# Loading an expert's input weights as bf16 from GpSimd's queue, and holding two loads of x until the band sums are taken

## The chip, the cores and the metric

The kernel runs on one core of one Trainium2 chip. A core has TensorE (matrix products into PSUM), VectorE, ScalarE and GpSimd (elementwise work), SyncE (which here issues transfers), and 16 DMA engines that all queues share. The metric is the time of one execution on the device, in microseconds: the median over three runs of the kernel before is 724.11 (723.76 to 725.01). The profiled execution spans 721.8 us.

## The reference

The input x is 8 x 4096 x 192 in fp32, the convolution's weights are 8 x 7, w_in is 192 x 2048 and w_out 2048 x 192. What is computed:

```
w    = softmax(weight, axis=-1)                  # 8 heads x 7 taps
y[s] = sum over k of w[head, k] * x[s + k - 6]   # causal, per head of 24 columns, zeros before each sequence
h    = y @ w_in                                  # 32768 x 2048
g    = h * cos(h)
out  = g @ w_out                                 # 32768 x 192, fp32
```

## The kernel before

Tokens are handled in units of 1024 (`U`), read in blocks of 128, and in tiles of 512 (`T`), two tiles to a unit. For a unit the steps are: load x as fp32 (`load_unit`, L72, with `load_edges`, L68, for the rows that reach back into earlier blocks); cast it to bf16 on GpSimd (`cast_unit`, L179); convolve it on TensorE by a product with a banded matrix `band` (L194; L292 for the first half of unit 0); copy the result out of PSUM as `ct`, doubled along its columns (L209, L251, or at once in L298); and turn it so that the 192 columns of the model lie on partitions (`cT`), by a transposing transfer on SyncE (L257), or for the first half of unit 0 by TensorE against an identity (L314, L317).

For a tile, eight steps j of matmul 1 (`mm1`, L350) multiply cT by a pair of blocks of 128 columns of w_in (`w`, bf16), ScalarE takes the cosine (L357), VectorE multiplies (L361), and matmul 2 (L380) works with w_out (`wo`, bf16) and `g`. The two halves of w_in's columns lie on partitions 0 to 63 and 64 to 127, and the two matmuls of a step use one half of TensorE's rows each. Outputs are copied by ScalarE (L392) and stored by SyncE.

The order of the work on each engine is written out by hand: `manual_schedule()` keeps the order of the program, and the strings `PE_FIRST`, `PE_ORDER`, `ACT_FIRST` and `ACT_ORDER` (L403 to L408) set how steps of matmul 1 (`h0` to `h7`), pieces of convolution (`c`, `d`, and `r` for `conv_rest`) and steps of matmul 2 (`m`) follow one another in a tile. Each engine[...] works strictly in the order of issue. A `nop` on SyncE with a dependence (L302) makes the transfers behind it wait for the named instruction.

The opening, which the change touches, goes like this before it:

- SyncE issues the first half of unit 0's x, then the first half of w_in in fp32 (`load_w(0)`, L84), then the second half of unit 0. ScalarE issues the second half of w_in (L118) and later unit 1 with its edges (L150, L151).
- TensorE runs products with zeros (`keep_warm`, L106) and spreads the convolution's weights to all partitions (L122). VectorE and ScalarE take the softmax of them (L145 to L156).
- GpSimd makes a mask of 32 partitions by two instructions (L130, L131) and copies it three times to the other partitions (L134). It then clears a block of `xb0`, and makes the identity (L137 to L140).
- VectorE multiplies mask and weights (`prod`, L270) and sums over the taps (`diag`, L273): these are the band sums. Sixteen small copies on three engines (L278) put them into `band`.
- ScalarE casts the first half of unit 0. TensorE convolves it (`conv_first`), and it is turned (`turn_first`). When its last copy is done, SyncE issues w_out in four transfers (L94).
- GpSimd casts the first quarter of w_in to bf16 (L280) as soon as it has landed, casts the second half of unit 0 (L281), casts the other three quarters of w_in (L334), and casts unit 1 (L335).
- The loop over tiles follows. In tile 0, `conv_rest` convolves the second half of unit 0; `double_unit` and `turn_unit` finish it, and then SyncE issues the load of unit 2 (L445) and GpSimd casts w_out in two pieces (L448).

Of the kernel before, what the change touches and what calls it, by code (L numbers as in the profile page):

```python
# [8 lines left out]
FP32 = mybir.dt.float32  # L9
BF16 = mybir.dt.bfloat16  # L10
AF = mybir.ActivationFunctionType
ALU = mybir.AluOpType
# [4 lines left out]
def kernel(  # L17
# [8 lines left out]
    nc = tc.nc  # L26
# [7 lines left out]
    NB = T // 128  # L34
    U = 1024
    NU = NTOK // U
    UB = U // 128
# [3 lines left out]
    NP = NF // 2  # L41
    NC = D // 64
# [4 lines left out]
    consts = ctx.enter_context(tc.tile_pool(name="consts", bufs=1))  # L47
# [20 lines left out]
    def load_edges(u, queue=nc.sync):  # L68
        queue.dma_start(out=x_tiles[u][:, UB, :],
                          in_=xf[u * U - 8 : u * U - 8 + U, :].rearrange("(n t) d -> n t d", t=128)[:, 0:16, :])  # L70

    def load_unit(u, n0=0, n1=UB, queue=nc.sync):  # L72
        if n0 == 0:
            x_tiles[u] = xin.tile([128, UB + 1, D], FP32, name="x_f")
        queue.dma_start(out=x_tiles[u][:, n0:n1, :],  # L75
                          in_=xf[u * U + n0 * 128 : u * U + n1 * 128, :].rearrange("(n p) d -> p n d", p=128))


    w_f = consts.tile([128, NC, NP, 128], FP32)
    w_src = moe_w_in.rearrange("(m k) (t f) -> t m k f", k=NC, t=2)  # L80
    HP = NP // 2

    def load_w(t, queue):
        queue.dma_start(out=w_f[64 * t : 64 * t + 64].rearrange("p k j f -> p k (j f)"), in_=w_src[t])  # L84

    load_unit(0, 0, NB)
    load_w(0, nc.sync)
    load_unit(0, NB, UB)
    wo_f = consts.tile([128, NP, 2, D], FP32)
    wo_src = moe_w_out.rearrange("(i j p) d -> p j i d", i=2, p=128)  # L90

    def load_wo(q):
        for i in range(2):
            nc.sync.dma_start(out=wo_f[:, q * HP : (q + 1) * HP, i], in_=wo_src[:, q * HP : (q + 1) * HP, i])  # L94
# [9 lines left out]
    def keep_warm(n, bank=idle):  # L104
        for _ in range(n):
            nc.tensor.matmul(out=bank, lhsT=zero[:, 0:128], rhs=zero, start=True, stop=True)  # L106
# [7 lines left out]
                            channel_multiplier=32)  # L114
    scrap = consts.tile([128, 1], FP32)
    nc.scalar.activation(out=scrap, in_=one, func=AF.Exp)  # L116

    load_w(1, nc.scalar)  # L118
    keep_warm(3)
    w_all = o_pools[1].tile([128, T], FP32, name="o_ps1")  # L120
    w_bc = w_all[:, 0 : HQ * K].rearrange("p (h k) -> p h k", k=K)
# [7 lines left out]
    mask = consts.tile([128, E, K], BF16)  # L129
    nc.gpsimd.memset(mask[0:32], 0.0)  # L130
    nc.gpsimd.affine_select(out=mask[0:32], in_=mask[0:32], compare_op=ALU.not_equal, fill=1.0, base=1 - K,  # L131
                            pattern=[[1, E], [1, K]], channel_multiplier=-1)
    for q in range(1, 4):
        nc.gpsimd.tensor_copy(out=mask[32 * q : 32 * q + 32], in_=mask[0:32])  # L134
    band = consts.tile([128, H, 256], BF16)
    nc.vector.memset(band, 0.0)
    nc.gpsimd.memset(xb0[:, 0, :], 0.0)  # L137
    ident = consts.tile([128, 128], BF16)
    nc.gpsimd.memset(ident, 0.0)
# [7 lines left out]
    nc.vector.tensor_tensor(out=wexp, in0=w_bc, in1=wmax.to_broadcast([128, HQ, K]), op=ALU.subtract)  # L147
    nc.scalar.activation(out=wexp, in_=wexp, func=AF.Exp)
    nc.scalar.activation(out=scrap, in_=one, func=AF.Sin)
    load_unit(1, queue=nc.scalar)  # L150
    load_edges(1, queue=nc.scalar)  # L151
    wsum = consts.tile([128, HQ, 1], FP32)
    nc.vector.tensor_reduce(out=wsum[:, :, 0], in_=wexp, axis=mybir.AxisListType.X, op=ALU.add)
    winv = consts.tile([128, HQ, 1], FP32)
    nc.vector.reciprocal(winv, wsum)
    nc.vector.tensor_tensor(out=wn, in0=wexp, in1=winv.to_broadcast([128, HQ, K]), op=ALU.mult)  # L156
    w = consts.tile([128, NC, NP, 128], BF16)
    wo = consts.tile([128, NP, 2, D], BF16)


    sync_dep = mybir.DependencyInfo(mybir.DependencyClass.Sync, mybir.DependencyReason.DATA)
# [17 lines left out]
    def cast_unit(u, n0=0, n1=UB + 1, copy=nc.gpsimd.tensor_copy):  # L179
        bf[u] = xb0 if u == 0 else xbf_pool.tile([128, UB + 1, D], BF16, name="x_bf")  # L180

        o = 1 if u == 0 else 0
        copy(out=bf[u][:, n0 + o : n1 + o, :].rearrange("p n (h k r) -> p (n h) k r", k=NC, r=R),  # L183
             in_=x_tiles[u][:, n0:n1, :].rearrange("p n (h r k) -> p (n h) k r", k=NC, r=R))
        if u and u % UPS == 0:
            nc.gpsimd.memset(bf[u][0:8, UB, :], 0.0)
        bf.pop(u - 2, None)
# [27 lines left out]
    def o_banks():  # L215
        return [o_pools[b].tile([128, T], FP32, name="o_ps%d" % b) for b in range(2)]
# [52 lines left out]
    prod = consts.tile([128, HQ, E, K], BF16)  # L269
    nc.vector.tensor_tensor(out=prod, in0=mask.rearrange("p (o e) k -> p o e k", o=1).to_broadcast([128, HQ, E, K]),  # L270
                            in1=wn.rearrange("p h (o k) -> p h o k", o=1).to_broadcast([128, HQ, E, K]), op=ALU.mult)
    diag = consts.tile([128, HQ, E], FP32)
    nc.vector.tensor_reduce(out=diag, in_=prod, axis=mybir.AxisListType.X, op=ALU.add)  # L273

    three = {"D": nc.vector.tensor_copy, "A": nc.scalar.copy, "P": nc.gpsimd.tensor_copy}
    for i, k in enumerate("DPDPDPADPDPADPAD"):
        q, rows = divmod(i, 4)
        three[k](out=band[32 * rows : 32 * rows + 32, HQ * q : HQ * (q + 1), 32 * rows : 32 * rows + E],  # L278
                     in_=diag[32 * q : 32 * q + 32])
    nc.gpsimd.tensor_copy(out=w[:, :, 0:2], in_=w_f[:, :, 0:2])  # L280
    cast_unit(0, NB, UB)  # L281
    ct_tiles[0] = ct_pool.tile([128, UB + 1, NC, 2, 64], BF16, name="ct")
    cT[0] = cT_pool.tile([128, UB + 1, NC, 128], BF16, name="cT")
# [2 lines left out]
    def conv_first():  # L286

        banks = o_banks()
        for half in range(2):
            for h in range(H):  # L290
                for prev in range(2):
                    nc.tensor.matmul(  # L292
                        out=banks[half][:, 0 : 2 * D].rearrange("p (n k h r) -> p h n k r", n=2, k=NC, h=H)[:, h],
                        lhsT=band[:, h, 128 * prev : 128 * prev + 128],
                        rhs=bf[0][:, 2 * half + 1 - prev : 2 * half + 3 - prev, h * G : (h + 1) * G].rearrange(
                            "p n (k r) -> p n k r", k=NC),
                        start=(h == 0 and prev == 0), stop=(h == H - 1 and prev == 1), skip_group_check=True)
            m = copies[half](out=ct_tiles[0][:, 2 * half : 2 * half + 2].rearrange("p n k t w -> p (n k) t w"),  # L298
                             in_=banks[half][:, 0 : 2 * D].rearrange("p (m t w) -> p m t w", t=1, w=64).to_broadcast(
                                 [128, 2 * NC, 2, 64]))  # L300

        tc.add_manual_dep(nc.sync.nop().ins, m.ins.name, sync_dep, reason="order of the transfers")  # L302
        load_wo(0)
        load_wo(1)

    def turn_first(half):
        for n in range(2):
            last = half and n
            ps = [o_pools[0].tile([128, T], FP32, name="o_ps0")] if last else ring_banks()
            if n == 0:  # L310
                keep_warm(2 - half, ps[1])
            ps = ps[0]
            for k in range(NC):
                nc.tensor.matmul(out=ps[:, k * 128 : (k + 1) * 128],  # L314
                                 lhsT=ct_tiles[0][:, 2 * half + n, k, :, :].rearrange("p t w -> p (t w)"), rhs=ident,
                                 start=True, stop=True, skip_group_check=True)
            copies[n](out=cT[0][:, 2 * half + n].rearrange("p c k -> p (c k)"), in_=ps[:, 0 : NC * 128])  # L317

    def conv_rest():
# [6 lines left out]
        for b in range(2):  # L326
            for c in range(2):
                conv_out(0, c, [x[:, 4 * G * 2 * c :] for x in banks], NB, NB, UB, copies[1 - b], banks=(b,))

    conv_first()  # L330
    turn_first(0)
    turn_first(1)
    for j in (2, 4, 6):
        nc.gpsimd.tensor_copy(out=w[:, :, j : j + 2], in_=w_f[:, :, j : j + 2])  # L334
    cast_unit(1)  # L335


# [181 lines left out]
```

## Time and profile before

| What | Value |
|---|---|
| Median of three runs | 724.11 us |
| Span of the profiled execution | 721.8 us |
| TensorE busy | 709.3 us, 98% |
| VectorE busy | 611.2 us, 85% |
| ScalarE busy | 617.0 us, 85% |
| GpSimd busy | 152.6 us, 21% |
| Moved by transfers | 86.03 MB, mean 119 GB/s |
| Cast of w_in's first quarter (L280), starts at | 12.58 us |
| First product of matmul 1 (L350), starts at | 13.46 us |
| Cast of unit 1 (L183), starts at | 18.09 us |
| Load of unit 2 issued (L75), at | 23.04 us |

All times within a profile count from the start of its span. A line of the timeline gives start, length, engine, source line, operation, what it writes and reads with shapes, how many instructions are merged in it, and in brackets how long the engine had been idle before and what released it. A line of the chain gives start, length and the piece of work: the chain is followed back from the last instruction, at each step to what released it. A line of the stretches gives a window, then for each engine its busy time with the number of instructions, then the clock that TensorE was granted (1.00 is full), the share of the 16 DMA engines that was busy, and the GB/s that they moved. PE is TensorE, PEld its weight loads, DVE VectorE, ACT ScalarE, POOL GpSimd, SPq the queue of SyncE.

### The profile page before, as it was taken

The page shows a single profiled execution, that of the slowest core. Times are in us where ns is not written, and L with a number is a line of the kernel's source. Part 1 is how long each engine was busy: PE and PEld are TensorE (multiplying, and loading weights), DVE is VectorE, ACT ScalarE, POOL GpSimd, SP SyncE. Part 2 cuts the span into 40 slices and gives each one's busy share as a digit, 9 for nine tenths or more (in the row PEclk, how much of TensorE's full clock was granted, in tenths as well). Part 3 has the DMA queues.
Part 4 walks back from the last instruction along what each step waited for, and adds up shares of the span by engine and source line. Part 5 has one row for each costly group of instructions (what it writes and reads, how often), then busy time and mean ns, then how long its engine had stood idle before and what let it go on. Part 6 is the DMA issues. An engine that isn't in the chain of part 4 may idle for free.

```text
span 721.8 us, 26319 instructions
## 1 busy us (share of the span) xinstructions
PE 709.3 (98%) x11826; PEld 530.9 (74%) x11827; DVE 611.2 (85%) x535; ACT 617.0 (85%) x779; POOL 152.6 (21%) x129
## 2 busy tenths in 40 slices
PE   7899999999999999999999999999999999999997
PEld 3577777777777777777777777777777777777776
DVE  5878888888888888888888888888888888888884
ACT  5888888888888888888888888888888888888884
POOL 5731122210222210222210222210222211221000
PEclk9999999999999999999999999999999999999999
DMA  9855434555443556444555343566443555324312
GB/s 232 206 123 144 106 111 94 123 144 143 104 113 92 126 143 141 97 123 91 127 144 139 104 116 89 130 144 131 109 119 86 135 143 131 108 74 81 87 46 67
DMA packets 183665, 86.03 MB, mean 119 GB/s; under 512 B 111617, under 2 KB 183169, under 8 KB 183553
## 3 DMA queue, kind: packets, MB, share of 16 engines
q1 hardware_dynamic: 182160, 82.69, 47.1%
q10 hardware_dynamic: 1392, 1.67, 0.9%
q8 instruction: 92, 1.51, 0.9%
q14 instruction: 21, 0.16, 0.1%
HBM read 31.36 MB, written 25.17 MB: 78 GB/s over the span
## 4 chain that ended last, share of the span: by engine, by line
PE 95%; DMA 2%; POOL 1%; issue 0%; SPq 0%; ACT 0%; DVE 0%; DVEq 0%; POOLq 0%
PE o_ps L380 46%; PE h L350 45%; PE h L194 3%; DMA x_f<-in_x_dram 2%; POOL x_bf L183 1%; PE h L380 0%; POOL w L334 0%; POOL wo L448 0%; SPq L75 0%; DVE g L361 0%; DVEq L514 0%; ACT cs L357 0%; ACT o_sb L392 0%; POOL ct L251 0%; SPq L84 0%
## 5 line engine op out<-in xcount | busy, mean ns | idle before, releaser
L361 DVE TENSOR_TENSOR g<-h,cs 128x1024 bf16<-128x1024 f32 (+1 forms) x513 | 603.6, 1218 | 97.2 <-ACT cs L357 92.3
L357 ACT ACTIVATE cs<-h 128x1024 bf16<-128x1024 f32 (+1 forms) x513 | 511.6, 1026 | 63.0 <-PE h L350 55.8
L380 PE MATMUL o_ps<-wo,g 64*128 64x192 bf16 x8128 | 423.8, 243 | 1.7 <-ACT o_sb L392 0.6
L380 PEld LDWEIGHTS <-g 64*128 64x128 bf16 x8192 | 362.2, 94 | 86.0 <-SPq L168 1.2
L350 PE MATMUL h<-cT,w 64*128 64x512 bf16 (+1 forms) x3078 | 399.5, 377 | 3.4 <-POOL w L280 3.3
L350 PEld LDWEIGHTS <-w 64*128 64x128 bf16 x3078 | 155.0, 94 | 88.8 <-POOL w L280 3.5
L263 POOL COPY cT<-cT 128x144 bf16<-128x144 bf16 x31 | 9.5, 307 | 495.5 <-DMA cT<-ct 392.0
L183 POOL CAST x_bf<-x_f 128x1728 bf16<-128x1728 f32 (+1 forms) x32 | 80.6, 2518 | 4.7 <-DMA x_f<-in_x_dram 4.4
L209 ACT CAST ct<-h 128x432 bf16<-128x432 f32 x120 | 56.4, 522 | 27.8 <-PE h L194 27.2
L392 ACT COPY o_sb<-o_ps 128x384 f32<-128x384 f32 x127 | 60.2, 474 | 4.9 <-PE o_ps L380 4.9
L251 POOL COPY ct<-ct 128x1728 bf16<-128x1728 bf16 (+1 forms) x32 | 51.3, 1603 | 19.4 <-ACT ct L209 19.1
L194 PE MATMUL h<-x_bf,band 64*128 64x216 bf16 (+1 forms) x472 | 42.7, 254 | 1.0 <-POOL x_bf L183 1.0
L194 PEld LDWEIGHTS <-band 64*128 64x128 bf16 (+1 forms) x496 | 22.5, 95 | 6.4 <-issue 3.8
L106 PE MATMUL o_ps<-zero 128*128 128x512 bf16 x12 | 5.3, 610 | 1.3 <-DVE zero L101 1.3
L380 PE MATMUL h<-wo,g 64*128 64x192 bf16 x64 | 5.8, 243 | 0.0
L106 PEld LDWEIGHTS <-zero 128*128 128x128 bf16 x15 | 1.7, 127 | 3.6 <-issue 2.2
L194 PE MATMUL o_ps<-x_bf,band 128*128 128x96 bf16 (+1 forms) x24 | 2.3, 253 | 1.3 <-POOL x_bf L183 1.3
L448 POOL CAST wo<-wo_f 128x1536 bf16<-128x1536 f32 x2 | 2.9, 1476 | 0.0
L209 ACT CAST ct<-o_ps 128x432 bf16<-128x432 f32 (+1 forms) x6 | 2.4, 461 | 0.2
L116 ACT ACT_TABLE_LOAD x1 | 1.3, 1283 | 1.4 <-PEq L503 1.4
L392 ACT COPY o_sb<-h 128x384 f32<-128x384 f32 x1 | 0.5, 478 | 2.4 <-PE h L380 2.4
L334 POOL CAST w<-w_f 128x768 bf16<-128x768 f32 x3 | 2.4, 832 | 0.0
(47 smaller groups left out, 27.8 us busy)
## 6 DMA issues: line engine op xcount, KB each, us to landing
out_dram<-o_sb SPq DMA_DIRECT2D x63, 384.0 KB
x_f<-in_x_dram SPq DMA_DIRECT2D x30, 768.0 KB
x_f<-in_x_dram SPq DMA_DIRECT2D x30, 96.0 KB
wo_f<-in_moe_w_out_dram SPq DMA_DIRECT2D x4, 384.0 KB
x_f<-in_x_dram SPq DMA_DIRECT2D x2, 384.0 KB
w_f<-in_moe_w_in_dram SPq DMA_DIRECT2D x1, 768.0 KB
w_f<-in_moe_w_in_dram ACTq DMA_DIRECT2D x1, 768.0 KB
x_f<-in_x_dram ACTq DMA_DIRECT2D x1, 768.0 KB
```

The lines of the kernel that those rows point to most:

```text
L106: nc.tensor.matmul(out=bank, lhsT=zero[:, 0:128], rhs=zero, start=True, stop=True)
L183: copy(out=bf[u][:, n0 + o : n1 + o, :].rearrange("p n (h k r) -> p (n h) k r", k=NC, r=R), in_=x_tiles[u][:, n0:n1, :].rearrange("p n (h ...
L194: return nc.tensor.matmul(out=ps[i // 2][:, 0 : (n1 - n0) * 2 * G].rearrange("p (n k i r) -> p i n k r", n=n1 - n0, k=NC, i=2)[:, i % 2], ...
L209: copy(o[:, :, 0, :], i[:, :, 0, :])
L251: nc.gpsimd.tensor_copy(out=ct[:, n0:n1, :, 1, :], in_=ct[:, n0:n1, :, 0, :])
L263: nc.gpsimd.tensor_copy(out=cT[u][:, 0:UB, :, 0 : K - 1], in_=cT[u][:, UB].rearrange("p c (n t) -> p n c t", t=16)[:, :, :, 8 : 8 + K - 1])
L350: nc.tensor.matmul(out=h[:, i, n0 * 128 : n1 * 128], lhsT=w[rows, k, j, :], rhs=c[rows, m0 + n0 : m0 + n1, k, :], start=(k == 0), stop=(k ...
L357: nc.scalar.activation(out=cs[:, :, part], in_=h[:, :, part], func=AF.Sin, bias=math.pi / 2.0, scale=1.0)
L361: nc.vector.tensor_tensor(out=g_tiles[t][:, 2 * j : 2 * j + 2, part], in0=h[:, :, part], in1=cs[:, :, part], op=ALU.mult)
L380: m = nc.tensor.matmul(out=o_ps[tt, b][:, si * D : (si + 1) * D], lhsT=g_tiles[tt][rows, f, s * 128 : (s + 1) * 128], rhs=wo[rows, f // 2, ...
L392: nc.scalar.copy(o_sb[t][:, 2 * b : 2 * b + 2, :].rearrange("p s d -> p (s d)"), o_ps.pop((t, b))[:, 0 : 2 * D])
L448: nc.gpsimd.tensor_copy(out=wo[:, q * HP : (q + 1) * HP], in_=wo_f[:, q * HP : (q + 1) * HP])
```

## The change

It changes how the opening's transfers are made and ordered:

- `w` is loaded straight as bf16 by two transfers on GpSimd's queue, which read fp32 from memory and write bf16; the fp32 tile `w_f` and its four casts on GpSimd (L280, L334) go.
- The three copies of the mask go from GpSimd to VectorE (one) and ScalarE (two), so that GpSimd reaches its transfers sooner.
- The second half of unit 0, unit 1 and its edges are all issued by SyncE, and only after the band sums (a `nop` on SyncE that depends on the sum of L273), so that the bytes of w_in go ahead of them.

Line numbers in the text are those of the kernel before.

```diff
--- before.py
+++ after.py
@@ -76,16 +76,15 @@
                           in_=xf[u * U + n0 * 128 : u * U + n1 * 128, :].rearrange("(n p) d -> p n d", p=128))
 
 
-    w_f = consts.tile([128, NC, NP, 128], FP32)
+
+    w = consts.tile([128, NC, NP, 128], BF16)
     w_src = moe_w_in.rearrange("(m k) (t f) -> t m k f", k=NC, t=2)
     HP = NP // 2
 
-    def load_w(t, queue):
-        queue.dma_start(out=w_f[64 * t : 64 * t + 64].rearrange("p k j f -> p k (j f)"), in_=w_src[t])
+    def load_w(t):
+        nc.gpsimd.dma_start(out=w[64 * t : 64 * t + 64].rearrange("p k j f -> p k (j f)"), in_=w_src[t])
 
     load_unit(0, 0, NB)
-    load_w(0, nc.sync)
-    load_unit(0, NB, UB)
     wo_f = consts.tile([128, NP, 2, D], FP32)
     wo_src = moe_w_out.rearrange("(i j p) d -> p j i d", i=2, p=128)
 
@@ -114,8 +113,6 @@
                             channel_multiplier=32)
     scrap = consts.tile([128, 1], FP32)
     nc.scalar.activation(out=scrap, in_=one, func=AF.Exp)
-
-    load_w(1, nc.scalar)
     keep_warm(3)
     w_all = o_pools[1].tile([128, T], FP32, name="o_ps1")
     w_bc = w_all[:, 0 : HQ * K].rearrange("p (h k) -> p h k", k=K)
@@ -130,10 +127,12 @@
     nc.gpsimd.memset(mask[0:32], 0.0)
     nc.gpsimd.affine_select(out=mask[0:32], in_=mask[0:32], compare_op=ALU.not_equal, fill=1.0, base=1 - K,
                             pattern=[[1, E], [1, K]], channel_multiplier=-1)
-    for q in range(1, 4):
-        nc.gpsimd.tensor_copy(out=mask[32 * q : 32 * q + 32], in_=mask[0:32])
     band = consts.tile([128, H, 256], BF16)
     nc.vector.memset(band, 0.0)
+    for q, copy in enumerate((nc.vector.tensor_copy, nc.scalar.copy, nc.scalar.copy)):
+        copy(out=mask[32 * q + 32 : 32 * q + 64], in_=mask[0:32])
+    for t in range(2):
+        load_w(t)
     nc.gpsimd.memset(xb0[:, 0, :], 0.0)
     ident = consts.tile([128, 128], BF16)
     nc.gpsimd.memset(ident, 0.0)
@@ -147,14 +146,11 @@
     nc.vector.tensor_tensor(out=wexp, in0=w_bc, in1=wmax.to_broadcast([128, HQ, K]), op=ALU.subtract)
     nc.scalar.activation(out=wexp, in_=wexp, func=AF.Exp)
     nc.scalar.activation(out=scrap, in_=one, func=AF.Sin)
-    load_unit(1, queue=nc.scalar)
-    load_edges(1, queue=nc.scalar)
     wsum = consts.tile([128, HQ, 1], FP32)
     nc.vector.tensor_reduce(out=wsum[:, :, 0], in_=wexp, axis=mybir.AxisListType.X, op=ALU.add)
     winv = consts.tile([128, HQ, 1], FP32)
     nc.vector.reciprocal(winv, wsum)
     nc.vector.tensor_tensor(out=wn, in0=wexp, in1=winv.to_broadcast([128, HQ, K]), op=ALU.mult)
-    w = consts.tile([128, NC, NP, 128], BF16)
     wo = consts.tile([128, NP, 2, D], BF16)
 
 
@@ -270,14 +266,18 @@
     nc.vector.tensor_tensor(out=prod, in0=mask.rearrange("p (o e) k -> p o e k", o=1).to_broadcast([128, HQ, E, K]),
                             in1=wn.rearrange("p h (o k) -> p h o k", o=1).to_broadcast([128, HQ, E, K]), op=ALU.mult)
     diag = consts.tile([128, HQ, E], FP32)
-    nc.vector.tensor_reduce(out=diag, in_=prod, axis=mybir.AxisListType.X, op=ALU.add)
+    summed = nc.vector.tensor_reduce(out=diag, in_=prod, axis=mybir.AxisListType.X, op=ALU.add)
+
+    tc.add_manual_dep(nc.sync.nop().ins, summed.ins.name, sync_dep, reason="order of the transfers")
+    load_unit(0, NB, UB)
+    load_unit(1)
+    load_edges(1)
 
     three = {"D": nc.vector.tensor_copy, "A": nc.scalar.copy, "P": nc.gpsimd.tensor_copy}
     for i, k in enumerate("DPDPDPADPDPADPAD"):
         q, rows = divmod(i, 4)
         three[k](out=band[32 * rows : 32 * rows + 32, HQ * q : HQ * (q + 1), 32 * rows : 32 * rows + E],
                      in_=diag[32 * q : 32 * q + 32])
-    nc.gpsimd.tensor_copy(out=w[:, :, 0:2], in_=w_f[:, :, 0:2])
     cast_unit(0, NB, UB)
     ct_tiles[0] = ct_pool.tile([128, UB + 1, NC, 2, 64], BF16, name="ct")
     cT[0] = cT_pool.tile([128, UB + 1, NC, 128], BF16, name="cT")
@@ -298,7 +298,6 @@
             m = copies[half](out=ct_tiles[0][:, 2 * half : 2 * half + 2].rearrange("p n k t w -> p (n k) t w"),
                              in_=banks[half][:, 0 : 2 * D].rearrange("p (m t w) -> p m t w", t=1, w=64).to_broadcast(
                                  [128, 2 * NC, 2, 64]))
-
         tc.add_manual_dep(nc.sync.nop().ins, m.ins.name, sync_dep, reason="order of the transfers")
         load_wo(0)
         load_wo(1)
@@ -330,8 +329,6 @@
     conv_first()
     turn_first(0)
     turn_first(1)
-    for j in (2, 4, 6):
-        nc.gpsimd.tensor_copy(out=w[:, :, j : j + 2], in_=w_f[:, :, j : j + 2])
     cast_unit(1)
 
 
```

## The prediction

> **What bounds the kernel now.** I read the page's busy shares, then the chain of work that ended last, then the stretches of the first 23 us, then the order of instructions in them.
>
> ```profile
> PE 709.3 (98%) x11826; PEld 530.9 (74%) x11827; DVE 611.2 (85%) x535; ACT 617.0 (85%) x779; POOL 152.6 (21%) x129
> ...
> PE 95%; DMA 2%; POOL 1%; issue 0%; SPq 0%; ACT 0%; DVE 0%; DVEq 0%; POOLq 0%
> ```
>
> TensorE carries 95% of the chain. The change touches none of its matmuls, so it is worth what it moves the opening, where the chain is not on TensorE. In order of time that part reads (start, length, what):
>
> ```profile
> 2.06 12.51 DMA x_f<-in_x_dram
> 14.57 0.05 issue
> 14.62 1.22 POOL x_bf L183
> 15.84 1.53 POOL w L334 x2
> 17.38 0.72 issue
> 18.09 0.99 POOL x_bf L183
> ...
> 20.57 0.84 POOL ct L251
> ...
> 23.04 0.86 SPq L75
> ...
> 23.95 5.34 DMA x_f<-in_x_dram
> ...
> 29.44 2.54 POOL x_bf L183
> ...
> 32.02 0.53 PE h L194 x4
> ```
>
> Unit 0's second half lands at 14.57, GpSimd casts it, then casts three quarters of w_in (L334), then casts unit 1, doubles unit 0's ct, and only then can SyncE turn unit 0 and load unit 2 (23.04), which ends in the convolution at 32.02. From there TensorE runs nearly without a gap: whatever shifts 32.02 shifts the end. Beside it lies a second chain, which starts at w_in:
>
> ```profile
> 12.58 0.82 POOL L280 CAST w<-w_f 128x768 bf16<-128x768 f32 x1 [4.84 <-DMA w_f<-in_moe_w_in_dram]
> ...
> 13.46 2.73 PE L350 MATMUL h<-cT,w 64*128 64x256 bf16 x18 [3.29 <-POOL w L280]
> 14.30 1.24 ACT L357 ACTIVATE cs<-h 128x512 bf16<-128x512 f32 x2 [3.79 <-PE h L350]
> ```
>
> The last of w_in is in at about 12.55; with the first cast, matmul 1 starts at 13.46, though cT was ready near 10.5. Both chains wait for bytes. The stretches (engine columns, then granted clock, DMA share, GB/s) show how these flow:
>
> ```profile
> 4.00:8.00 4.00, 3.67 (x23) 1.47 (x22) 3.42 (x12) 3.33 (x6) 2.62 (x10) 1.00 1.00 210
> 8.00:12.00 4.00, 2.06 (x34) 1.27 (x35) 2.08 (x3) 1.75 (x3) 0.00 (x0) 1.00 1.03 225
> 12.00:20.00 8.00, 5.93 (x52) 3.18 (x53) 3.90 (x6) 4.63 (x8) 6.20 (x6) 0.79 1.09 312
> 20.00:23.00 3.00, 2.32 (x20) 1.09 (x19) 2.67 (x3) 2.92 (x6) 3.00 (x4) 1.00 0.15 35
> ```
>
> The DMA engines are full from 3 to 20 us. While w_in's 4 KB packets pass they move 210 to 225 GB/s; once only rows of x and w_out (768 B) are left, 312. The clock's 0.79 hides 0.50 between 14 and 16 us, after TensorE's idle 3.29.
>
> **What the skill says.** (1) "DMA: Bandwidth & Descriptors", section "SWDGE vs HWDGE vs iDMA": a cast in transit must be issued from GpSimd, whose cores write the descriptors in software. No transfer before is of that kind. (2) Same page, "Anatomy of one DMA": about 2.0 us fixed plus bytes at 436 GB/s; "Specifications" puts the first byte about 1 us after issue. (3) "SBUF — State Buffer", section "Door 1: The DMA port swizzle": a destination of 64 partitions reaches half the ports, 196 GB/s measured at 1 MiB, and two such transfers side by side gain little. The 210 of w_in's stretch agrees, so the writing side may set its pace. (4) "TensorE: Matmul & The Clock Gate", "What's actually happening": about 3.4 us of idle halves the clock. The trace agrees (3.29 idle, then 0.50).
>
> **The change, part by part.**
>
> Removed from GpSimd: four casts of w_in, 0.82 + 2.38 us (L280, L334), both on the chains above, and three mask copies (1.29 us, L134).
>
> Mask copies: one on VectorE, two on ScalarE. From ScalarE's 32x76 copies (250 ns) and 128x384 (478 ns), 266 columns cost about 0.39 us; two from 3.06 end at 3.85, so the exponential at 3.74 slips 0.1 and the weights' normalisation with it. The mask product then starts at 4.8 instead of 4.68. Cost 0.1 us, hidden while w_in is awaited. VectorE's copy lies in its idle 1.01 before 3.33.
>
> The two transfers: GpSimd issues them from 3.05. Descriptor writing is not in the trace: lower bound about 0.5 us each (SyncE's and ScalarE's own issues take 0.45 to 0.68), upper 2.5 us (the fixed 2.0 and some for 192 rows). I take 1.0, so GpSimd is free at 5.1, does its two memsets and the identity (4.41 to 5.30 before, 0.9) by 6.0, and meets the band sums, now at 6.0 instead of 5.90. Behind a longer issue stand its six band copies (1.71 us), and behind them the first convolution.
>
> When w_in lands: unit 0's first half moves alone and is in by about 3.9, so w_in's bytes begin near 4.2. HBM is still read in fp32 (1.57 MB); only the 0.79 MB written is halved. Lower rate: 205 GB/s as now. Upper: 330, the rate of the small rows, if writing was the limit. I take 270, midway. The held transfers are issued from 6.0 and by the delay seen at the start (issue 0.82, bytes near 2.2) flow from 7.4. Until then w_in has moved 3.2 us x 270 = 0.86 MB. The other 0.71 MB shares the engines packet by packet: 4096 against 768 bytes gives w_in 84%, 227 GB/s, 3.1 us, so 10.5; with 0.4 us to signal, 10.9. At 205 it is 13.0, at 330 about 9.4, and then cT (10.4) limits.
>
> Chain of w_in: no cast follows, so matmul 1 starts at 11.0, 2.4 us earlier. TensorE's idle falls from 3.29 to under 1 us, the clock should stay at 1.0, and the first six half-width matmuls take about 0.45 us to ScalarE's start instead of 0.84. ScalarE then does halves a and b in 1.24 us and step 1 from about 12.7 instead of 16.22. That is 3.5 us.
>
> Chain of x: the second half of unit 0 gets 16% until 10.5 (0.13 MB), the other 0.26 MB at 326 GB/s ends at 11.3; signal and cast 11.7 to 12.9 (15.84 before). Unit 1 with its edges, 0.88 MB at 326, ends at 14.0, with signal and the small rows 14.6. GpSimd casts it from 14.6 instead of 18.09: 3.5 us earlier. This holds only because L334's casts, which kept GpSimd until 18.1, are gone. Doubling, turning and load of unit 2 follow at the same distances: load at 19.5 instead of 23.04. w_out is queued behind unit 1 on SyncE and needs 1.57 MB / 327 = 4.8 us, so it is in by 19.5; its second cast on GpSimd, due about 19.3, waits little.
>
> Sum: both chains give 3.5 us. I take off 0.3 for w_out at the casts and for six band copies slipping a little: 3.2. 724.1 - 3.2 = 720.9 us.
>
> **The rivals.**
>
> (a) The pace is kept: a narrower write frees nothing and w_in lands at 13.0; or descriptors take 2.5 us each, GpSimd is free for band copies at 9.0, and cT comes at 13. For: 210 GB/s may be the reading side, and the trace has no such issue. Against: small rows read at 312 from the same memory. Matmul 1 at about 13.1 gains 0.3; unit 1's cast at about 16.6 gains 1.5, of which the later of the two chains lets through about 0.8: 723.3 us.
>
> (b) Casting halves the engines' pace, to about 130 GB/s of reading. By 7.4 w_in has 0.42 MB; 1.15 MB at 109 GB/s take 10.5 us: 18.3 with the signal. Matmul 1 slips 4.8 us; unit 1 lands near 21.3, 3.2 us later than its cast now. With GpSimd's saved casts the end moves by about 4: 728 us. For: one queue now carries both halves, nothing of unit 1 flows before 7.4, and no transfer of before converts. Against: the page prices GpSimd's transfers at the same 436 GB/s as any.
>
> (c) The upper rate: w_in at 9.4, cT limits, matmul 1 at 10.4, step 1 of ScalarE 4.1 earlier: 720.0. In the same direction as the forecast.
>
> **How the numbers follow.** Forecast with (c): 0.70 ((c) is 0.15 of it); (a) 0.16; (b) and other losses of the opening 0.14. The measured time is the forecast's, 720.9. The low end is (c) with half a microsecond to spare, 719.5; the high end takes in (a) and the milder half of (b), 725.8. By 0.2% (1.45 us: 722.7 and 725.6) these give faster 0.70, same 0.16, slower 0.14.
>
> **What would show it.** Right: matmul 1 (L350) starts between 10.4 and 12, its releaser the transfer of w_in or cT; the clock stays at 1.0 from 13 to 17; GpSimd's cast of unit 1 starts at 14 to 15.5 with the transfer as its releaser; the convolution now at 32.02 starts near 28.5; the stretch 5 to 10 us shows more than 225 GB/s read. Wrong in (a): L350 after 12.7, the clock at 0.5, or band copies of GpSimd (L278) starting after 7. Wrong in (b): L350 after 15. I would also be wrong if unit 2's load (L75) did not move up with unit 1's cast, since then the saved opening would be given back at 29 us.

## The result, and the profile after

The changed kernel takes 720.39 us (720.15 to 720.73) against 724.02 for the kernel before: 3.6 us less, ratio 0.9948 with a 95% interval of 0.9931 to 0.9965. Run again beside another kernel on one chip it took 720.50 against 723.96, ratio 0.9953 (0.9941 to 0.9966). The forecast was 720.9. The two profiled executions span 719.0 and 721.8 us, 2.8 apart.

In the code after, the cast of a unit is L179, the convolution L190, matmul 1 L347, the cosine L354, the band copies L279, and the transfers of w_in L85. The part of the timeline around w_in and the cast of unit 1:

```profile
2.96 1.40 POOL L85 DMA_DIRECT2D w<-in_moe_w_in_dram  x2
...
10.44 1.65 PE L347 MATMUL h<-cT,w 64*128 64x256 bf16 x18 [0.18 <-DVE cT L316]
11.15 2.00 ACT L354 ACTIVATE cs<-h 128x512 bf16<-128x512 f32 x3 [0.54 <-PE h L347]
...
11.92 1.21 POOL L179 CAST x_bf<-x_f 128x768 bf16<-128x768 f32 x1 [4.09 <-DMA x_f<-in_x_dram]
...
15.05 2.51 POOL L179 CAST x_bf<-x_f 128x1728 bf16<-128x1728 f32 x1 [1.91 <-DMA x_f<-in_x_dram]
...
18.36 1.54 SPq L253 DMA_TRANSPOSE cT<-ct  x1
...
19.95 0.90 SPq L75 DMA_DIRECT2D x_f<-in_x_dram  x1
...
29.15 0.53 PE L190 MATMUL h<-x_bf,band 128*128 128x216 bf16 x4 [1.09 <-POOL x_bf L179]
```

Matmul 1 starts at 10.44 instead of 13.46, and what it waited for last is no longer the cast of w_in but VectorE's copy of cT: w_in came just in time. GpSimd's cast of unit 1 starts at 15.05 instead of 18.09, and what it waits for is now the transfer, where before the cast stood behind those of w_in. Unit 2's load goes out 3.1 us earlier, and the convolution of unit 2 starts 2.9 us earlier, still waiting 1.09 us for its cast. The part of the chain that leads there:

```profile
10.14 7.09 DMA wo_f<-in_moe_w_out_dram
...
17.51 0.82 POOL ct L247
18.33 1.42 POOL wo L445
19.75 0.14 SPq L253
...
19.95 0.90 SPq L75
...
20.91 5.52 DMA x_f<-in_x_dram
...
26.58 2.54 POOL x_bf L179
...
29.15 0.53 PE h L190 x4
```

From the load at 19.95 on it is the chain of before, three microseconds earlier. The chain's releasers are inferred, and w_out in its first line need not be taken at its word: the doubling (L247) stands behind GpSimd's cast of unit 1, which ended at 17.56 and had waited for x. The stretches (engine columns, granted clock, DMA share, GB/s):

```profile
4.00:8.00 4.00, 3.80 (x20) 1.38 (x18) 3.43 (x12) 3.48 (x7) 2.76 (x10) 1.00 0.92 119
8.00:12.00 4.00, 3.73 (x53) 2.25 (x53) 2.29 (x4) 2.61 (x5) 0.08 (x1) 1.00 1.07 282
12.00:20.00 8.00, 5.37 (x58) 2.81 (x58) 6.31 (x9) 6.55 (x11) 5.83 (x4) 1.00 0.94 263
```

The clock stays at 1.00. The 119 GB/s of the first stretch must be read with care: for a transfer that casts, this column counts the bytes written. The page counts 0.79 MB for w_in's queue while HBM still read 31.36 MB, as before. In bytes read, w_in's 1.57 MB passed between about 4.5 and 10.0, some 285 GB/s.

### The profile page after: what moved, and what is told of

It reads as the page before. It is cut to its first block, busy times and chain, and to the rows that moved or that the text cites. A ratio compares the mean times of both kernels' runs of the same rounds, so it can differ in the third digit from the quotient of the medians.

```text
span 719.0 us, 26316 instructions
## 1 busy us (share of the span) xinstructions
PE 708.1 (98%) x11827; PEld 529.9 (74%) x11827; DVE 611.1 (85%) x536; ACT 617.7 (86%) x781; POOL 149.7 (21%) x124
## 3 DMA queue, kind: packets, MB, share of 16 engines
HBM read 31.36 MB, written 25.17 MB: 79 GB/s over the span
## 4 chain that ended last, share of the span: by engine, by line
PE 95%; DMA 2%; POOL 1%; ACT 1%; DVE 0%; issue 0%; SPq 0%; DVEq 0%; POOLq 0%
PE o_ps L377 46%; PE h L347 45%; PE h L190 3%; DMA wo_f<-in_moe_w_out_dram 1%; DMA x_f<-in_x_dram 1%; PE h L377 0%; POOL x_bf L179 0%; POOL wo L445 0%; ACT L148 0%; DVE g L358 0%; PE o_ps L292 0%; DVEq L511 0%; ACT x_bf L179 0%; ACT cs L354 0%; POOL mask L128 0%
## 5 line engine op out<-in xcount | busy, mean ns | idle before, releaser
L354 ACT ACTIVATE cs<-h 128x1024 bf16<-128x1024 f32 (+1 forms) x513 | 511.3, 1026 | 59.3 <-PE h L347 52.2
L347 PE MATMUL h<-cT,w 64*128 64x512 bf16 (+1 forms) x3078 | 398.2, 376 | 0.3 <-DVE cT L316 0.2
L347 PEld LDWEIGHTS <-w 64*128 64x128 bf16 x3078 | 154.4, 94 | 85.6 <-issue 1.1
L179 POOL CAST x_bf<-x_f 128x1728 bf16<-128x1728 f32 (+1 forms) x32 | 80.5, 2515 | 8.7 <-DMA x_f<-in_x_dram 8.6
L247 POOL COPY ct<-ct 128x1728 bf16<-128x1728 bf16 (+1 forms) x32 | 51.2, 1601 | 18.9 <-ACT ct L205 18.2
L190 PE MATMUL h<-x_bf,band 64*128 64x216 bf16 (+1 forms) x472 | 42.7, 254 | 1.1 <-POOL x_bf L179 1.1
L190 PEld LDWEIGHTS <-band 64*128 64x128 bf16 (+1 forms) x496 | 22.2, 94 | 7.4 <-issue 4.8
L190 PE MATMUL o_ps<-x_bf,band 128*128 128x96 bf16 (+1 forms) x24 | 1.9, 223 | 2.6 <-POOL x_bf L179 2.6
```

The source lines that it names most:

```text
L190: return nc.tensor.matmul(out=ps[i // 2][:, 0 : (n1 - n0) * 2 * G].rearrange("p (n k i r) -> p i n k r", n=n1 - n0, k=NC, i=2)[:, i % 2], ...
L247: nc.gpsimd.tensor_copy(out=ct[:, n0:n1, :, 1, :], in_=ct[:, n0:n1, :, 0, :])
L347: nc.tensor.matmul(out=h[:, i, n0 * 128 : n1 * 128], lhsT=w[rows, k, j, :], rhs=c[rows, m0 + n0 : m0 + n1, k, :], start=(k == 0), stop=(k ...
L354: nc.scalar.activation(out=cs[:, :, part], in_=h[:, :, part], func=AF.Sin, bias=math.pi / 2.0, scale=1.0)
```

## The experiments

Ratios are to the kernel before, measured on the same chip, and its median there lay between 723.83 and 723.96; differences in us are between medians, and 720.4 stands for the changed kernel. A trace shows one execution of each kernel.

**Without the hold.** Unit 0's second half follows its first half at once, unit 1 goes out on ScalarE's queue as before the change.

```diff
     load_unit(0, 0, NB)
+    load_unit(0, NB, UB)
...
+    load_unit(1, queue=nc.scalar)
+    load_edges(1, queue=nc.scalar)
...
-    tc.add_manual_dep(nc.sync.nop().ins, summed.ins.name, sync_dep, reason="order of the transfers")
-    load_unit(0, NB, UB)
-    load_unit(1)
-    load_edges(1)
```

> The changed kernel without the hold: unit 0's second half goes out right behind its first half on SyncE, unit 1 and its edges on ScalarE as before the change. Theory (the hold puts w_in's bytes first): some of x's bytes go ahead of w_in or share with it, matmul 1 starts near 11.5 to 12 instead of 10.44, and the time is 0.5 to 1 us above the changed kernel, near 721.2. Rival (w_in's queue takes the engines from x whatever is issued, as in the changed profile, where no packet of x passes between 6 and 9 us): matmul 1 at 10.4 to 11, x lands no later, time within 0.3 us of the changed kernel or below it.

Measured: 722.67 us, ratio 0.9981 (0.9973 to 0.9988): 2.3 us of the gain are gone. From its timeline and its stretches:

```profile
12.95 2.42 PE L346 MATMUL h<-cT,w 64*128 64x256 bf16 x17 [2.24 <-DMA w<-in_moe_w_in_dram]
...
14.00:16.00 2.00, 2.00 (x16) 1.03 (x13) 1.33 (x2) 1.27 (x3) 1.54 (x1) 0.50 1.10 325
```

TensorE had started at 10.45 with a single matmul, whose rows lie in the half of w_in loaded first (it landed at about 9.1), and then waited 2.24 us for the other half (about 12.9); its clock was halved again after that. Packets of unit 1 passed between 7 and 12 us among those of w_in (203 against 30 from 7 to 8). Unit 1's cast began at 14.46, earlier than the 15.05 of the changed kernel, so here it is the late matmul 1 that costs, not a late x. The theory holds, at more than twice the size expected. This is so for most executions, not for all: of 22 runs two took 719.32 and 719.49, less than any run of the changed kernel, with a mean clock of 0.999, and the other 20 took 721.26 to 723.84. What went otherwise in the two no trace shows.

**The hold alone, on the kernel before.** w_in stays fp32 on SyncE and ScalarE, with GpSimd's casts.

```diff
     load_w(0, nc.sync)
-    load_unit(0, NB, UB)
...
-    load_unit(1, queue=nc.scalar)
-    load_edges(1, queue=nc.scalar)
...
+    tc.add_manual_dep(nc.sync.nop().ins, summed.ins.name, sync_dep, reason="order of the transfers")
+    load_unit(0, NB, UB)
+    load_unit(1)
+    load_edges(1)
```

> The kernel before with the hold alone: w_in still fp32 on SyncE and ScalarE with GpSimd's casts, unit 0's second half and unit 1 issued by SyncE after the band sums. Theory (the cast in transit and the casts it saves carry the gain): w_in's 1.57 MB at about 210 GB/s from 3.9 land near 11.4, the first cast follows, matmul 1 starts near 12.3, 1.1 us earlier than before; unit 1's cast still waits for GpSimd's casts of w_in, so the end gains 0.5 to 1.2 us: 723.2. Rival (the order of the transfers carries the gain): matmul 1 near 11.3 and 721.5 or less.

Measured: 723.21 us, ratio 0.9992 (0.9984 to 1.0000). From its timeline:

```profile
13.09 0.82 POOL L281 CAST w<-w_f 128x768 bf16<-128x768 f32 x1 [5.34 <-DMA w_f<-in_moe_w_in_dram]
...
13.97 2.74 PE L351 MATMUL h<-cT,w 64*128 64x256 bf16 x18 [3.79 <-POOL w L281]
...
17.34 2.52 POOL L180 CAST x_bf<-x_f 128x1728 bf16<-128x1728 f32 x1
```

The time is the theory's, its way is not: matmul 1 started half a microsecond later than in the kernel before (13.46), so w_in did not come sooner. What moved up is unit 1's cast, at 17.34 instead of 18.09. Order alone gives nearly nothing. With the engines almost to itself w_in moved at 199 to 221 GB/s (4 to 10 us), no faster than the 210 to 225 that the engines moved before, with x beside it, and a few last packets of its second half still passed among those of x between 11 and 12.5. Why these came so late was not found.

**The mask copies back on GpSimd**, ahead of its transfers.

```diff
-    for q, copy in enumerate((nc.vector.tensor_copy, nc.scalar.copy, nc.scalar.copy)):
-        copy(out=mask[32 * q + 32 : 32 * q + 64], in_=mask[0:32])
+    for q in range(3):
+        nc.gpsimd.tensor_copy(out=mask[32 * q + 32 : 32 * q + 64], in_=mask[0:32])
```

> The changed kernel with the three mask copies back on GpSimd, ahead of its two transfers (1.3 us later at issue). Theory (w_in lands at about 10.1, just when cT is ready, so the later issue comes through nearly whole): matmul 1 starts at 11.3 to 11.6 and the end moves by 0.5 to 1.2 us, near 721.3. Rival (unit 2's load sets the end and there is slack in front of matmul 1): matmul 1 late by 1 us but the time within 0.3 us of the changed kernel.

Measured: 721.93 us, ratio 0.9976 (0.9966 to 0.9985). The 1.3 us of later issue cost 1.5 us. Matmul 1's second matmul waited for w_in until 12.15, and unit 1's cast slipped from 15.05 to 16.49. There is no slack in front of w_in's issue; the rival falls. The loss came by the chain of x all the same: in the trace unit 2's convolution starts at 30.19, 1.0 us later, and waits for GpSimd's cast.

**fp32 on the same queue.** Queue, order and hold are the changed kernel's; only the cast in transit is undone.

```diff
+    w_f = consts.tile([128, NC, NP, 128], FP32)
...
-        nc.gpsimd.dma_start(out=w[64 * t : 64 * t + 64].rearrange("p k j f -> p k (j f)"), in_=w_src[t])
+        nc.gpsimd.dma_start(out=w_f[64 * t : 64 * t + 64].rearrange("p k j f -> p k (j f)"), in_=w_src[t])
...
+    nc.gpsimd.tensor_copy(out=w[:, :, 0:2], in_=w_f[:, :, 0:2])
     cast_unit(0, NB, UB)
...
+    for j in (2, 4, 6):
+        nc.gpsimd.tensor_copy(out=w[:, :, j : j + 2], in_=w_f[:, :, j : j + 2])
     cast_unit(1)
```

> The changed kernel with w_in kept in fp32 on GpSimd's queue and cast by GpSimd as before the change (first quarter ahead of unit 0's second half, the rest ahead of unit 1): queue, order and hold are the changed kernel's, only the cast in transit is undone. Theory (the halved write quickens the transfer): w_in reads at about 210 GB/s instead of 280, lands near 11.9, matmul 1 starts near 12.8, unit 1's cast near 17.5: 723 us. Rival (the queue and the order set the pace, and the reading side limits it): w_in lands near 10.2 as in the changed kernel, matmul 1 at 11.1; what is lost is the casts alone, 1 to 2 us: 721.5 to 722.3.

Measured: 724.16 us, ratio 1.0006 (0.9998 to 1.0014): without the cast in transit everything else in the change is worth nothing. The stretches show the pace of w_in alone on the engines:

```profile
6.00:8.00 2.00, 1.72 (x15) 0.66 (x13) 1.75 (x7) 1.50 (x4) 1.46 (x6) 1.00 1.05 211
8.00:10.00 2.00, 1.90 (x34) 1.27 (x35) 1.22 (x2) 1.23 (x2) 0.00 (x0) 1.00 1.05 227
```

211 to 227 GB/s, read and written alike, from the same memory, on the same queue and in as many packets (416) as the cast's 285 of reading. So it is the halved write that quickens the transfer, not the queue, and the reading side was not the limit. That the 64 partitions written to are the reason, as the prediction supposes, no run here shows. w_in's first cast could start only at 13.46, later than in the kernel before (12.58), where w_in was issued at 1.33 and 1.50 instead of from 2.96 on.

**Unit 2's load ahead of the turning of unit 0.**

```diff
             elif k == "r":
+                load_unit(2)
+                load_edges(2)
                 conv_rest()
                 double_unit(0, NB, UB)
                 turn_unit(0, NB, UB)
-                load_unit(2)
-                load_edges(2)
```

> The changed kernel with unit 2's load and edges issued by SyncE before the turning of unit 0 instead of after it. Theory (the end hangs on unit 2's landing: the convolution at 29.15 waits 1.09 us for its cast, and the load is issued only at 19.95 behind the turning): unit 2 lands by 22, its cast starts behind the doubling of unit 1 near 24.2, the convolution starts near 28.1, gain about 1 us: 719.4. Rival (w_in's chain through ScalarE and VectorE sets the end too): within 0.3 us of the changed kernel. Second rival: the transposing transfer of unit 0 now queues behind 0.86 MB of unit 2 and delays tile 1, no gain or a loss of up to 1 us.

Measured: 725.34 us, ratio 1.0015 (1.0006 to 1.0025): all of the gain lost and more. The second rival is right, and larger than it said. From the timeline of one of the slowest runs (726.53):

```profile
18.20 4.42 SPq L253 DMA_TRANSPOSE cT<-ct  x1
...
25.10 1.46 PE L347 MATMUL h<-cT,w 64*128 64x512 bf16 x6 [2.76 <-DMA cT<-ct]
```

Unit 2 was in early (its cast began at 23.96). But the turning behind it, issued at 18.20, landed only at 25.1, and tile 1 needs it. TensorE sat idle for 2.76 us and then worked at a clock of 0.50 until about 34:

```profile
28.00:30.00 2.00, 2.00 (x12) 1.31 (x9) 0.89 (x1) 0.83 (x1) 1.40 (x1) 0.50 0.00 0
30.00:32.00 2.00, 2.00 (x14) 1.37 (x14) 1.22 (x1) 0.19 (x1) 1.11 (x1) 0.50 0.00 0
```

The runs spread from 722.02 to 726.65 and follow the mean clock: 722.02 at 0.999, 723.58 and 724.62 at 0.997, 724.54 to 725.77 at 0.994, 725.79 to 726.65 at 0.992. So most of the 5 us goes with the halved clock; 1.6 us were lost in the one run that nearly kept it. The late load that the chain shows is the price of a turning that must go first.

**Without w_in.** The two transfers are left out and the tile is filled with a constant, so w_in is missing from the output.

```diff
-    for t in range(2):
-        load_w(t)
...
+    nc.gpsimd.memset(w, 0.01)
     cast_unit(0, NB, UB)
```

> The changed kernel without the two transfers of w_in: it is left out, and the tile is filled with a constant by GpSimd after its band copies, so the output lacks w_in. It shows what w_in's transfer still costs. Theory (cT, not w_in, now limits matmul 1; x is held up by w_in's bytes until 9.4): matmul 1 starts at 10.3 to 10.5 as now, unit 0's second half lands near 9 and unit 1's cast starts near 12 instead of 15.05; the end gains 1 to 2 us through unit 2's earlier load: 718.5 to 719.5. Rival (ScalarE's and VectorE's chain from 11.15 on sets the end): gain under 0.5 us.

Measured: 718.33 us, ratio 0.9924 (0.9912 to 0.9935): w_in's bytes still cost 2.1 us. Matmul 1 starts at 10.58, no earlier than with w_in, so this is not a wait of matmul 1. It is x that comes sooner:

```profile
12.77 2.55 POOL L177 CAST x_bf<-x_f 128x1728 bf16<-128x1728 f32 x1 [0.97 <-DMA x_f<-in_x_dram]
...
24.14 2.55 POOL L177 CAST x_bf<-x_f 128x1728 bf16<-128x1728 f32 x1 [2.44 <-DMA x_f<-in_x_dram]
```

Unit 1's cast is 2.3 us earlier than in the changed kernel and unit 2's 2.4 us; the time is 2.1 us less. In the changed kernel it is the chain of x that sets the end of the opening.

**Doubling unit 0's second half in the copies out of PSUM**, so that the turning no longer stands behind GpSimd's cast of unit 1.

```diff
-                conv_out(0, c, [x[:, 4 * G * 2 * c :] for x in banks], NB, NB, UB, copies[1 - b], banks=(b,))
+                conv_out(0, c, [x[:, 4 * G * 2 * c :] for x in banks], NB, NB, UB, copies[1 - b], double=True, banks=(b,))
...
-                double_unit(0, NB, UB)
```

> The changed kernel with the doubling of unit 0's second half done by the four copies out of PSUM themselves (ScalarE and VectorE, two each) and GpSimd's doubling copy of it gone, so that the turning of unit 0 and unit 2's load behind it no longer wait for GpSimd's cast of unit 1. Theory (unit 2's late load is what still sets the end, and the turning must stay ahead of it): turning near 15.5, load of unit 2 near 17.2 instead of 19.95, its cast near 24.2 behind GpSimd's doubling of unit 1, convolution of unit 2 near 28, 0.7 to 1.1 us gained less 0.3 for the longer copies: 719.5 to 720. Rival (a transposing transfer in flight with the rows of w_out or unit 2 loses its pace, as when unit 2 went first): cT of unit 0 lands late, tile 1 waits, 721 us or more.

Measured: 720.01 us, ratio 0.9949 (0.9937 to 0.9962). The turning was issued at 15.50, as expected, but among w_out's rows its issue held SyncE for 2.57 us instead of 1.54, and unit 2's load went out at 18.17, not 17.2. The convolution of unit 2 started at 28.10, 1.05 us earlier, and it now waited for VectorE's product g, no longer for its cast. The profiled executions are 0.9 us apart (719.87 against 720.73), the medians only 0.4, within what the intervals can tell.

**GpSimd's doubling ahead of its cast of unit 1.**

```diff
-    cast_unit(1)
...
                 double_unit(0, NB, UB)
+                cast_unit(1)
```

> The changed kernel with GpSimd's doubling of unit 0's second half ahead of its cast of unit 1. Theory: turning near 15.8, load of unit 2 near 17.4, unit 1's cast 0.8 us later (15.8), so its convolution starts near 18.4 instead of 17.61 and ScalarE's and VectorE's chain loses 0.3 to 0.5: time 719.8 to 720.4. Rival as for the doubling in the copies: the transposing transfer among other rows is late, 721 us or more.

Measured: 720.87 us, ratio 0.9963 (0.9950 to 0.9977), above what was expected: unit 2's cast began 1.1 us earlier (25.52), but unit 1's convolution started at 18.38, 0.8 us late, and in the end that of unit 2 stood at 29.24, where it was, waiting for VectorE.

**Only unit 1 held.** Unit 0's second half follows its first half at once.

```diff
     load_unit(0, 0, NB)
+    load_unit(0, NB, UB)
...
     tc.add_manual_dep(nc.sync.nop().ins, summed.ins.name, sync_dep, reason="order of the transfers")
-    load_unit(0, NB, UB)
     load_unit(1)
```

> The changed kernel with unit 0's second half not held (it follows the first half at once on SyncE); unit 1 and its edges stay held. Theory (holding unit 1 is what keeps w_in ahead; the second half's 0.39 MB mostly fits into the time before w_in's first bytes at 4.5): w_in lands 0.6 us later, near 11, matmul 1 at 11.1; unit 0's second half is in by 6, its convolution no longer waits, unit 1 lands 0.5 us earlier; time within 0.5 us of the changed kernel, 719.9 to 720.9. Rival (any row of x ahead of w_in costs what the kernel without the hold lost): matmul 1 near 12.9, 722 us or more.

Measured: 719.25 us, ratio 0.9939 (0.9927 to 0.9952), better than expected. From the timeline:

```profile
7.89 1.23 POOL L180 CAST x_bf<-x_f 128x768 bf16<-128x768 f32 x1
10.44 1.62 PE L347 MATMUL h<-cT,w 64*128 64x256 bf16 x18 [0.18 <-DVE cT L316]
11.99 0.85 PE L191 MATMUL o_ps<-x_bf,band 128*128 128x96 bf16 x16
...
13.53 2.54 POOL L180 CAST x_bf<-x_f 128x1728 bf16<-128x1728 f32 x1 [4.40 <-DMA x_f<-in_x_dram]
...
18.46 0.95 SPq L75 DMA_DIRECT2D x_f<-in_x_dram  x1
```

The second half's bytes passed until about 4.8 us, where the changed kernel moved 55 GB/s (4 to 5 us), and w_in was still there at 10.44. The convolution of the second half follows matmul 1's first steps at once (11.99, where it waited till 13.19), and unit 1's cast and unit 2's load come 1.5 us earlier. Against the kernel without any hold it differs by unit 1 alone, which is held and goes out on SyncE's queue instead of ScalarE's: that is worth 3.4 us between the medians.

**Both edits**: unit 0's second half not held, and the doubling in the copies.

> Both edits: unit 0's second half not held, and the doubling in the copies. Theory: conv of the second half goes right after matmul 1's first steps near 12.3, its turning near 14, unit 2's load near 15.8[...]; the end is then set by ScalarE's and VectorE's chain: 719.3 to 720. Rival (transposing among other rows is slow): 721 us or more.

Measured: 719.08 us, ratio 0.9935 (0.9922 to 0.9947), no more than the one above by itself.

**The changed kernel and the one that holds only unit 1, on one chip.**

> The changed kernel itself once more, on one chip with the next run, so that the two can be compared directly: 720.2 to 720.6, ratio to the kernel before near 0.995.

> The changed kernel with unit 0's second half not held, unit 1 still held, once more beside the changed kernel. Theory (holding unit 0's second half costs about 1 us, since it fits into the time before w_in's first bytes): 0.9 to 1.3 us below the changed kernel, 719.1 to 719.5. Rival (the two differ by the chip they ran on): within 0.4 us of it.

Measured: 720.50 (720.45 to 720.73) and 719.32 (719.29 to 719.69). The difference is 1.2 us, with no overlap of the runs: holding unit 1 alone beats both kernels.

**The runs together.** In all fourteen profiled executions, the kernel before and the changed one among them, the time of the execution less the start of unit 2's convolution (the first product of a convolution that writes `h`) is 691.5 to 691.8 us, while that start runs from 26.78 (without w_in) to 34.81 (unit 2's load first). So every variant wins or loses before this convolution, and what releases it says which chain counts. In the kernel before, in the changed one, with the mask copies on GpSimd and with unit 1 alone held, it waits for GpSimd's cast of unit 2, the chain of x. Where matmul 1 is late (without the hold, the hold alone, fp32) and where x is earlier (the two doublings, both edits, without w_in) it waits 0.49 us for VectorE's g, the chain of matmul 1. (With unit 2's load first it waits for neither.) After the change the two lie close: with x moved up by the doubling in the copies the start went from 29.15 to 28.10, and with unit 1 alone held from 27.64 to 27.49.

## Why the prediction was right

The mechanism was right, and the sizes were near.

*Chain of w_in.* The two issues took 1.40 us together, 0.7 each; 1.0 was taken, with bounds of 0.5 and 2.5. The upper bound took over the fixed cost of a whole transfer, but what holds GpSimd is the issue alone. w_in's first bytes came at about 4.45, 1.5 us after the first issue began, where 4.2 was reckoned. The band sums came 0.1 us later, as reckoned. w_in was taken at 270 GB/s of reading and did 285, and was in when TensorE asked for it at 10.44, where 10.9 was reckoned. Matmul 1 then waited for cT, which was the case of the upper rate: 10.44 against 11.0. The clock stayed at 1.0, but that was worth little by itself, since x set the end: three later runs of the kernel before show a mean clock of 1.0 and took 723.15, 723.85 and 723.86, where the medians are 723.86 and 723.96. The reason given for the pace, that the writing side had set it, was shown by keeping fp32 on the same queue (211 to 227).

*Chain of x.* Unit 1's cast was put at 14.6 and came at 15.05; unit 2's load at 19.5 and came at 19.95; the convolution at 28.5 and came at 29.15. The prediction had both chains give 3.5 us; by the profiles that of w_in gave more (4 us at ScalarE's step 1: about 12.1 instead of 16.22) and that of x 3.0, and the one that gave less set the end. The earlier start of matmul 1 had to come too, as the kernel without the hold shows, but it did not set the size of the gain. That the time fell within 0.5 us of the forecast was in part luck: 0.3 us were taken off for w_out at the casts and for the band copies, which cost next to nothing on the path, while the convolution came 0.65 us later than reckoned.

*The step that failed* is the sharing: "w_in 84%, 227 GB/s". In the kernel before, the queues of SyncE and ScalarE did share packet for packet (46 against 47 from 9 to 10 us, 0.04 MB of x against 0.19 of w_in). With w_in on GpSimd's queue it was otherwise: between 6 and 9 us not one packet of x passed, though unit 0's second half was issued at about 6.0; its first came after 9, when w_in's last were going. It did no harm to the sum, since x then ran at 360 GB/s and was in by 11.9 instead of 11.7. But it hid what the hold costs: issued early, the second half is nearly through when w_in's first bytes come, as the kernel that holds only unit 1 shows. The prediction had unit 0's first half in by 3.9 and w_in's bytes from 4.2, and did not ask what else could pass before them.

*The sign* of "more than 225 GB/s read" from 5 to 10 us was badly put, since the profile counts what such a transfer writes. And w_out's second cast waited 1.36 us, not "little", but the chain shows nothing on the path behind it.

*The rivals.* (a) fell: the pace of 285 lay above the middle of its bounds and the issue near its better one. (b) fell: casting did not slow the engines in bytes read. What the parts are worth, from the runs: without the cast in transit nothing is left; without the hold 1.2 us are left; without the move of the mask copies, 1.9. The losses, 3.8, 2.3 and 1.5 us, add up to twice the gain of 3.6, so the parts overlap: leaving one out takes some of the others' gain with it.

## What to carry to other kernels

Where an opening waits for a weight that is cast after loading, casting it in transit can pay twice: the casts go from the engine, and the transfer itself quickens if its writing side set its pace (here 211 to 227 GB/s in fp32, 285 of reading in bf16). Hold back only those transfers that would flow at the same time as the urgent one: a transfer that fits into the time before its first bytes is free, and holding that too cost 1.2 us here. And when the chain shows a late load, look at what it is queued behind before you move it: here the transfer ahead of it was needed sooner, and the swap cost 5 us between the medians. Two chains that lie close together limit each other: shortening one gains only up to where the other ends, here about a microsecond.

## What the runs showed of the hardware

- A transfer of x issued from SyncE while w_in's packets were passing on GpSimd's queue did not share with them: it started about when they ended (none between 6 and 9 us, the first after 9.25). In the kernel with fp32 on GpSimd's queue it was issued at about 6 us and moved nothing before 11; without w_in in the way it was moving from 7.1 on. Where unit 1 was issued at 3.76 on ScalarE's queue it started near 7 and then did share, with 203 packets against 30 from 7 to 8 us. What decides this was not settled.
- A turning transfer issued behind 0.88 MB of x on the same queue took from 18.20 to 25.1 to land, and its issue held SyncE for 4.42 us instead of 1.54.
- TensorE's clock fell to 0.50 with waits of 3.29 us (the kernel before), 2.24 us (without the hold) and 2.76 us (unit 2's load first; the fall came at about 23.85, 1.5 us after the last product ended at 22.34). With GpSimd's doubling ahead of its cast a wait of 2.38 us left the clock at 1.00, so the length of the wait alone does not decide. The clock stayed at 0.50 for 3.4 us in the first two, and for 10.2 us, three times as long, in the third. The Trainium skill, "TensorE: Matmul & The Clock Gate", section "What's actually happening", names about 3.4 us of idle; the runs show that shorter waits can do it.
